# Scores of two groups in three by 32 keys on eight small tiles of the array in place of 64 keys on four, in a windowed attention and mixer kernel

## The chip, the core and the metric

The kernel runs on one core of a Trainium2 chip. The metric is the device time of one execution in microseconds. TensorE is called PE in the profile, VectorE DVE, ScalarE ACT, GpSimd POOL, SyncE SP.

## What is computed

The reference is an attention with a sliding window and a few sink keys, followed by an MLP mixer: first over tokens, then over channels. B, H, S, D are 4, 8, 768, 64; n_sink is 4 and window 128; the weights have 256 columns for tokens and 1536 for channels.

```python
scores = scale * np.matmul(q, k.transpose(0, 1, 3, 2))
keep = (pos[None, :] < n_sink) | ((rel >= 0) & (rel < window))   # rel = query - key
scores = np.where(keep, scores, -1000000000.0)
a = softmax(scores);  attn = a @ v
x = attn.transpose(0, 2, 1, 3).reshape(B, S, H * D)
xt = x.transpose(0, 2, 1)
h = np.maximum(xt @ w_tok1, 0.0) @ w_tok2
u = x + h.transpose(0, 2, 1)
out = u + np.maximum(u @ w_ch1, 0.0) @ w_ch2
```

## The kernel before

**Tiles.** Two heads of a batch are a pair; there are 16, pair p belonging to batch p // 4. The two heads (index i) lie in the two halves of 64 partitions of kT and qT, so a matmul for one head uses 64 rows of the array. S is six tiles of P = 128 (NT = 6). A key tile of 128 can only be seen by its own 128 queries and the next 128, so scores are kept as 128 keys by 256 queries; a group g is two such key tiles (k = 0, 1), and the groups 0, 1, 2 make a pair. The scores of one group fill one buffer of the tag "sc" in PSUM, `[P, i, k, 4, D]`: partitions are keys, then head, key tile, and 256 queries as four blocks of 64. There are two such buffers, and four banks of the tag "mx" for everything else.

**Scores** (`scores`, from line 547). The first four pairs, and group 0 of all pairs, go by_halves: for a key tile and a head one matmul with 64 rows and 128 keys as columns of the array, over 256 queries. Groups 1 and 2 of the pairs from 4 on go by_quarters: 64 keys are the columns (y = 0, 1), so that four tiles of 64x64 of the array work on the two heads and the two key halves, each over the 192 queries that can see its keys. The blocks that no matmul writes (the fourth for the first 64 keys, the first for the others) hold what was there; the exponential on ScalarE (line 587) reads all, and a multiplication by a 0/1 mask on VectorE (line 595) removes what is not kept. The last piece in the call of `piece` is the array's time in ns that the plan works with.

**Sink scores** (`score_sinks`, line 609). For two pairs at once, 32 keys of the first tile against queries 256 to 767: four matmuls on tiles of 64x32, 512 columns streamed.

**Turns.** q and k of pairs 5 to 7 are transposed by the array inside a burst (`transposed`, line 495) into a buffer of "sc" that is seen as bf16 (`turned_bank`), copied out, and then a memset clears one block of it (`cleared`, line 518), since its scores do not write that block. Pairs from 8 on are transposed by DMA from SP's queue. u of batch 1 is turned by the array in tiles of 64x64 (`turned_u` with `turn_quarters`, line 470), in the bursts of the scores of pairs 7 and 8; u of batches 2 and 3 goes by DMA transposes (`transfer_u`, line 853).

**Order.** Everything is emitted by a planner in the order in which each engine executes it. `first_attention` does the attention and token mixing of batch 0 by a list (FIRST_BATCH). Then there are two lists of units for TensorE: main, the channel mixers of batches 0 to 3 with 48 units each (24 of w_ch1, then 24 of w_ch2; a unit of w_ch1 is four matmuls over 384 columns), and side, the attention and token mixing of the batches 1 to 3 in 74 units. A burst is a side unit of several pieces, such as the scores of groups 1 and 2 of a pair, then turned u if there is any, then the sink scores if the pair's number is even. MERGED gives the order of the side units: "7/11" places unit 7 when 11 main units are out. `run` (line 338) takes each unit at the time at which the plan thinks that its inputs and PSUM banks are there, and gives the work that follows it (exponentials, copies, adds, loads) to the engine that is free first, by the costs written at each operation. On the chip each engine runs its instructions in this order and waits where an input is late.

**Loads.** POOL issues the loads of q, k (cast to bf16, two DMAs each), v and weights in the order of LOADS: T and A are w_tok1 and w_tok2, C0 to C3 quarters of w_ch1, D0 to D3 quarters of w_ch2. A load waits for its buffer (six of each of q, k, v).

Of the kernel before, what the change touches and what calls it, by code (L numbers as in the profile page):

```python
# [16 lines left out]
def kernel(  # L17
# [13 lines left out]
    nc = tc.nc  # L31
    B, H, S, D = q.shape
    P = 128
    NT = S // P
# [6 lines left out]
    NHP = H // 2  # L41
    HS = S // 2
    D1 = D + 1
# [1 line left out]


    MERGED = (
# [5 lines left out]
    )  # L53
    FIRST_BATCH = (
        "q0 k0 m00 s00 m01 s01 q1 m02 k1 s02 m11 x1 s11 m10 q2 s10 o01 m12 k2 s12 o00 m21 q3 s21 s20 k3 o11 "
# [1 line left out]
        "u21 t20 t30 u31 t31 t21"  # L57
    )
    LOADS = (
        "v1 v2 T0 v3 A0 k4 q4 C0 q5 C1 k5 q6 C2 k6 v4 v5 D0 q7 k7 C3 q8 v6 k8 D1 D2 D3 v7 q9 k9 v8 k10 v9 q10 "  # L60
        "v10 k11 q11 q12 q13 k12 k13 v11 k14 v12 q14 v13 v14 k15 q15 v15"
    )
    NQ = 6
    NPT = 3
# [17 lines left out]
    sc = [psum.tile([P, 2, 2, 4, D], FP32, name=f"ps_sc{n}", tag=f"sc{n}", bufs=1) for n in range(TAGS["sc"])]  # L82

    def bank(tag, *shape, dtype=FP32, slot=None):

        n = given[tag].pop(0) if slot is None else slot
        if tag == "sc":
            return sc[n]
        return psum.tile([P, *shape], dtype, name=f"ps_{tag}", tag=f"{tag}{n}", bufs=1)

    in_order = tc.keep_in_program_order
# [41 lines left out]
    def mm(*args, **kwargs):  # L133
        in_order(nc.tensor.matmul(*args, skip_group_check=True, **kwargs))  # L134
# [20 lines left out]
    tiles = {}  # L155
# [51 lines left out]
    ODD = D // 2  # L207
    v_sink_f = singles.tile([P, NHP, 2, D1], FP32)
    in_order(nc.vector.memset(v_sink_f, 0.0))  # L209
    for n in range(4):  # L210
        i, odd = n // 2, n % 2
        rows = slice(D * i + ODD * odd, D * i + ODD * odd + n_sink)
# [201 lines left out]
    def piece(ns, fn, deps, need, then, keys=()):  # L414
        op = Op({}, fn, deps, then, size=float(ns))
        op.need, op.keys = need, keys
        return op
# [100 lines left out]
    def cleared(key, readers):  # L518

        op = Op(  # L520
            {"DVE": 400.0}, lambda e: in_order(nc.vector.memset(tiles["ps_turned", key][0:D, :, :, 3], 0.0)), readers,
        )
        op.urgent = 2
        return op

    def width(g):
        return 3 * P if g == NT // 2 - 1 else 4 * P

    def of_keys(ps):
        return ps.rearrange("p i k b q -> p i (k b q)")  # L530
# [16 lines left out]
    def scores(p, g):  # L547

        by_pe = ("mask", p, g) in done
        quarters = p >= NHP and g > 0

        def by_halves(ps):
            for k in range(2):
                kt = 2 * g + k
                nq = 2 if kt < NT - 1 else 1
                for i in range(2):
                    mm(
                        of_keys(ps)[:, i, ds(2 * k * P, nq * P)], tiles["kT", p][ds(D * i, D), ts(kt, P)],  # L560
                        tiles["qT", p][ds(D * i, D), kt * P:(kt + nq) * P], start=not by_pe, stop=True,
                    )

        def by_quarters(ps):
            for k in range(2):
                for y in range(2):
                    a = 4 * g + 2 * k + y
                    nq = min(3, 2 * NT - a)
                    for i in range(2):
                        rows = ds(D * i, D)  # L570
                        mm(
                            ps[ds(D * y, D), i, k, y:y + nq], tiles["kT", p][rows, ts(a, D)],
                            tiles["qT", p][rows, D * a:D * (a + nq)], start=True, stop=True,
                        )

        def run():
            if ("pT", p) not in tiles:
                tiles["pT", p] = pTb[p % NPT]
            if not by_pe:
                tiles["ps_s", p, g] = bank("sc")  # L580
            (by_quarters if quarters else by_halves)(tiles["ps_s", p, g])

        def part(t):
            return t.rearrange("p i k n q -> p i (k n q)")[:, :, 0:width(g)]

        def exp(e):
            in_order(nc.scalar.activation(  # L587
                part(tiles["pT", p][:, :, ds(2 * g, 2)]), of_keys(tiles["ps_s", p, g])[:, :, 0:width(g)], AF.Exp,
                scale=scale,
            ))  # L590

        def mask(e):
            pt = part(tiles["pT", p][:, :, ds(2 * g, 2)])
            m = part(mask_first if g == 0 else mask_main)
            in_order(nc.vector.tensor_tensor(out=pt, in0=pt, in1=m, op=ALU.mult))  # L595

        x = done["exp", p, g] if by_pe else Op({}, None)
        x.cost, x.fn, x.deps = {"ACT": 190.0 + 1.5 * width(g)}, exp, [("pv", p - NPT)] if p >= NPT else []
        x.urgent = 2 * (p < NHP)
        then = [x]  # L600
        if not by_pe:
            then.append(Op({"DVE": 100.0 + 1.2 * width(g)}, mask, [x, done["masks"]]))
            then[-1].urgent = 2 * (p < NHP)
        done["p", p, g] = then[-1]
        deps = [*done["qT", p], *done["kT", p]] if g else [done["qT", p][0], done["kT", p][0]]
        deps += [done["mask", p, g]] if by_pe else []
        return piece((190, 165, 140)[g] if quarters else width(g) * 0.47, run, deps, {} if by_pe else {"sc": [[x]]}, then, [("s", p)])

    def score_sinks(p):


        def run():
            pT_sink = pTsb[p // 2 % 2]
            tiles["ps_sk", p] = bank("mx", (NT - 2) * P)
            for n in (p - 1, p):
                tiles["pT_sink", n] = pT_sink
                for i in range(2):
                    rows = ds(D * i, D)
                    c = ODD * (n % 2)
                    mm(  # L620
                        tiles["ps_sk", p][ds(D * i + c, ODD)], tiles["kT", n][rows, 0:ODD],
                        tiles["qT", n][rows, 2 * P:], start=True, stop=True,
                    )

        def exp(e):
            in_order(nc.scalar.activation(tiles["pT_sink", p], tiles["ps_sk", p], AF.Exp, scale=scale))

        x = Op({"ACT": 580.0}, exp, [("pv", n - 4) for n in (p - 1, p)] if p >= 4 else [])
        for n in (p - 1, p):
            done["p", n, NT] = x  # L630
        deps = [d for m in (p - 1, p) for d in [done["kT", m][0], *done["qT", m]]]
        return piece(320, run, deps, {"mx": [[x]]}, [x], [("sk", p - 1), ("sk", p)])

    def pv(p, half):
        b, hp = pairs[p]
# [251 lines left out]
    def first_attention():  # L887


        for p in range(NHP):  # L890
            prepare(p)
        made, names = {}, FIRST_BATCH.split()
        for p in range(NHP):
            for n in range(2):
                made["qk"[n] + str(p)] = turn(p, n)
        for p in range(NHP):
            for g in range(NT // 2):
                if f"m{p}{g}" in names:
                    made[f"m{p}{g}"] = masked(p, g)
                made[f"s{p}{g}"] = burst(scores(p, g))  # L900
            if p % 2:
                made[f"x{p}"] = burst(score_sinks(p))
                for n in (p - 1, p):
                    for half in range(2):
                        made[f"o{n}{half}"] = pv(n, half)
        for ct in range(NC):
            made[f"h{ct}"] = mix_h(0, ct, 0, NTOK)
            for half in range(2):
                by_pe = f"y{ct}{half}" in names
                made["uy"[by_pe] + f"{ct}{half}"] = mix_u(0, ct, half * QH, QH, by_pe)  # L910
                made[f"t{ct}{half}"] = transpose_u(0, ct, half * QH, QH)
        return [[made[name] for name in names]]

    def attention_and_tokens():
# [5 lines left out]
        for p in range(first, last + 1):  # L920
            b, hp = pairs[p]
            pieces = []
            if p < last:
                prepare(p + 1)
                if p + 1 < BY_DMA:
                    pieces.append(transposed(p + 1))
            pieces.append(scores(p, 0))
            if p > first:
                pieces.append(sink_values(p - 1))
# [6 lines left out]
            if p > first:  # L936
                units += [values(p - 1, i) for i in range(2)]
            pieces = [scores(p, 1), scores(p, 2)]
            if hp == 0 and p > first:
                units.append(mix_h(b - 1, 1, 0, NTOK))  # L940
# [228 lines left out]
```

## Time and profile before

| | us |
|---|---|
| median of 3 runs | 200.25 |
| lowest, highest | 199.9, 200.53 |
| the profiled execution, its own time | 200.4 |
| its span in the trace | 198.6 |

In the profile a busy time is the union of an engine's instructions, and PEld is the loading of weights, which runs beside the matmuls. A row of groups has the source line, engine, operation, output <- inputs by name, tile of the array (rows*columns), partitions x columns streamed, count, then busy us and mean ns of one, then idle time before them. Matmuls on different tiles of the array overlap, and a record holds the whole passage through the array, so the mean ns of one is longer than the step from one to the next. A few per cent of the matmul records can be missing. A row of the timeline has the start in us, the length from the first start to the last end, the group and its count (the shape named is that of the first). The chain is the work that ended last, followed back.

### The profile page before, as it was taken

The page shows a single profiled execution, that of the slowest core. Times are in us where ns is not written, and L with a number is a line of the kernel's source. Part 1 is how long each engine was busy: PE and PEld are TensorE (multiplying, and loading weights), DVE is VectorE, ACT ScalarE, POOL GpSimd, SP SyncE. Part 2 cuts the span into 40 slices and gives each one's busy share as a digit, 9 for nine tenths or more (in the row PEclk, how much of TensorE's full clock was granted, in tenths as well). Part 3 has the DMA queues.
Part 4 walks back from the last instruction along what each step waited for, and adds up shares of the span by engine and source line. Part 5 has one row for each costly group of instructions (what it writes and reads, how often), then busy time and mean ns, then how long its engine had stood idle before and what let it go on. Part 6 is the DMA issues. An engine that isn't in the chain of part 4 may idle for free.

```text
span 198.6 us, 4863 instructions
## 1 busy us (share of the span) xinstructions
PE 191.5 (96%) x2041; PEld 115.5 (58%) x2059; DVE 101.8 (51%) x224; ACT 105.5 (53%) x182; POOL 68.0 (34%) x86
## 2 busy tenths in 40 slices
PE   6998999999999999999999999999999999999993
PEld 1345995566655665566546755656655645564453
DVE  4578875688675465251646965606346431001222
ACT  4699767887735225887653554886610105772000
POOL 6099889779529624863530000000000000000000
PEclk9999999999999999999999999999999999999999
DMA  6999999999999999999999975100015161000223
GB/s 194 251 285 173 176 183 173 175 174 177 195 136 158 123 243 160 192 181 118 156 131 185 205 167 122 53 3 2 0 53 135 53 171 70 0 0 0 109 106 106
DMA packets 92358, 26.28 MB, mean 132 GB/s; under 512 B 82352, under 2 KB 89392, under 8 KB 92336
## 3 DMA queue, kind: packets, MB, share of 16 engines
q0 software_dynamic: 67232, 11.80, 76.5%
q1 hardware_dynamic: 25104, 14.17, 33.7%
q8 instruction: 16, 0.26, 0.5%
q14 instruction: 6, 0.05, 0.1%
HBM read 26.75 MB, written 6.29 MB: 166 GB/s over the span
## 4 chain that ended last, share of the span: by engine, by line
PE 90%; POOL 4%; DMA 3%; DVE 1%; issue 1%; SPq 1%; POOLq 0%
PE ps_mx L134 82%; PE ps_sc L134 5%; DMA v_sink_f<-in_v_dram 3%; POOL v_aug L127 2%; POOL w_tok L152 1%; PE ps_mx L137 1%; PE ps_sc L503 1%; SPq L213 1%; PE ps_mx L487 0%; PE ps_mx L475 0%; POOL k_bf L143 0%; POOL q_bf L143 0%; POOL v_sink L143 0%; DVE v_sink_f L209 0%; DVE mask_add L178 0%
## 5 line engine op out<-in xcount | busy, mean ns | idle before, releaser
L134 PE MATMUL ps_mx<-uT,w_ch 128*128 128x384 bf16 x384 | 66.6, 326 | 0.0
L134 PE MATMUL ps_mx<-w_ch,v1T 128*128 128x512 bf16 (+2 forms) x297 | 65.2, 362 | 0.9 <-issue 0.3
L587 ACT ACTIVATE pT<-ps_sc 128x1024 bf16<-128x1024 f32 (+1 forms) x48 | 44.2, 954 | 22.7 <-PE ps_sc L134 22.5
L147 ACT ACTIVATE v1T<-ps_mx 128x384 bf16<-128x384 f32 x80 | 39.3, 491 | 27.0 <-PE ps_mx L134 15.5
L134 PEld LDWEIGHTS <-w_ch 128*128 128x128 bf16 x384 | 36.0, 98 | 23.7 <-issue 0.9
L134 PEld LDWEIGHTS <-v1T 128*128 128x128 bf16 x312 | 28.5, 98 | 27.7 <-issue 0.5
L1005 DVE TENSOR_TENSOR o_sb<-ps_mx,u_sb 128x512 f32<-128x512 f32 x23 | 15.9, 691 | 40.9 <-PE ps_mx L134 38.9
L119 POOL DMA_DIRECT2D q_bf<-in_q_dram x24 | 19.9, 834 | 9.3 <-DMA v_aug<-in_v_dram 6.6
L119 POOL DMA_DIRECT2D k_bf<-in_k_dram x24 | 19.8, 831 | 7.8 <-DMA v_aug<-in_v_dram 2.0
L134 PEld LDWEIGHTS <-w_tok 128*128 128x128 bf16 x240 | 19.5, 98 | 4.8 <-issue 0.2
L804 DVE TENSOR_TENSOR u_sb<-ps_mx,x_sb 128x512 bf16<-128x512 f32 (+1 forms) x24 | 15.2, 655 | 13.1 <-PE ps_mx L134 13.1
L127 POOL DMA_DIRECT2D v_aug<-in_v_dram x16 | 16.8, 1052 | 9.7 <-PE ps_mx L134 5.5
L149 DVE TENSOR_SCALAR v1T<-ps_mx 128x384 bf16<-128x384 f32 x16 | 8.6, 550 | 19.9 <-PE ps_mx L134 19.7
L134 PEld LDWEIGHTS <-pT 128*128 128x128 bf16 x352 | 14.2, 98 | 2.7 <-issue 0.6
L595 DVE TENSOR_TENSOR pT<-pT,mask_main 128x768 bf16<-128x768 bf16 (+1 forms) x25 | 14.7, 615 | 1.3 <-ACT pT L587 1.2
L134 PE MATMUL ps_mx<-v_aug,pT 128*128 128x65 bf16 x352 | 15.3, 194 | 0.0
L134 PE MATMUL ps_sc<-qT,kT 64*64 64x192 bf16 (+3 forms) x288 | 15.1, 252 | 0.1
L134 PE MATMUL ps_mx<-h1T,w_tok 128*128 128x256 bf16 (+1 forms) x120 | 13.9, 252 | 0.1
L147 ACT ACTIVATE h1T<-ps_mx 128x512 bf16<-128x512 f32 (+1 forms) x9 | 4.5, 503 | 17.4 <-PE ps_mx L134 17.4
L134 PEld LDWEIGHTS <-kT 64*64 64x64 bf16 (+2 forms) x320 | 7.5, 101 | 10.6 <-issue 8.8
L134 PE MATMUL ps_mx<-x_sb,w_tok 128*128 128x256 bf16 (+1 forms) x120 | 12.2, 251 | 0.0
L697 DVE TENSOR_TENSOR x_sb<-ps_mx,recip 128x384 bf16<-128x384 f32 x22 | 11.6, 548 | 0.1
(64 smaller groups left out, 120.2 us busy)
## 6 DMA issues: line engine op xcount, KB each, us to landing
out_dram<-o_sb SPq DMA_DIRECT2D x23, 256.0 KB, 4.5
v_aug<-in_v_dram POOLq DMA_DIRECT2D x16, 192.0 KB, 10.4
w_ch<-in_moe_w_ch_dram POOLq DMA_DIRECT2D x8, 384.0 KB, 7.7
k_bf<-in_k_dram POOLq DMA_DIRECT2D x24, 96.0 KB, 8.2
q_bf<-in_q_dram POOLq DMA_DIRECT2D x24, 96.0 KB, 8.7
q_f<-in_q_dram SPq DMA_DIRECT2D x4, 384.0 KB, 6.0
k_f<-in_k_dram SPq DMA_DIRECT2D x4, 384.0 KB, 6.3
w_tok<-in_moe_w_tok_dram POOLq DMA_DIRECT2D x2, 384.0 KB, 7.3
```

The lines of the kernel that those rows point to most:

```text
L119: in_order(nc.gpsimd.dma_start(out=out[:, h], in_=rows[:, h]))
L127: in_order(nc.gpsimd.dma_start(out=v_aug.rearrange("p i t d -> p (i t) d")[:, :, 0:D], in_=v[b].rearrange("h s d -> (h s) d")[2 * hp * S:2 ...
L134: in_order(nc.tensor.matmul(*args, skip_group_check=True, **kwargs))
L137: in_order(nc.tensor.transpose(out, in_, ident))
L147: in_order(nc.scalar.activation(out, in_, AF.Relu))
L149: in_order(nc.vector.tensor_scalar_max(out=out, in0=in_, scalar1=0.0))
L152: return in_order(nc.gpsimd.dma_start(out=out, in_=in_))
L587: in_order(nc.scalar.activation(part(tiles["pT", p][:, :, ds(2 * g, 2)]), of_keys(tiles["ps_s", p, g])[:, :, 0:width(g)], AF.Exp, scale=scale,
L595: in_order(nc.vector.tensor_tensor(out=pt, in0=pt, in1=m, op=ALU.mult))
L697: in_order(nc.vector.tensor_tensor(out=x_sb[b][:, :, ds((2 * hp + i) * D, D)], in0=tiles["ps_o", p, i][:, :, 0:D], in1=tiles["recip", p, i ...
L804: in_order(nc.vector.tensor_tensor(out=u_part(b, g, s0, n), in0=tiles["ps_u", b, g, s0], in1=x_sb[b][:, s0:s0 + n, c0:c0 + cn], op=ALU.add,))
L1005: in_order(nc.vector.tensor_tensor(out=o_sb.rearrange("p (g c) -> p g c", g=2), in1=u_rows(b, st), in0=tiles["ps_out", b, st].rearrange("p ...
```

## The change

In groups 1 and 2 of the pairs from 4 on, 32 keys (ODD = D // 2) are the columns of the array instead of 64. A key tile is then four strips c of 32 keys, and with the two heads a set is eight matmuls on eight tiles of 64x32, each over the 160 queries that can see its keys (fewer at the end of the sequence). A burst of both groups has 32 matmuls where it had 16. The strip that the memset clears is now columns 160 to 255 of partitions 0 to 63. The plan's costs of a group 2 (140 to 125) and of sink scores (320 to 230 from pair 4 on) change, and MERGED and LOADS are new lists of the same units and loads.

```diff
@@ -45,11 +45,11 @@
 
 
     MERGED = (
-        "0/0 1/2 2/3 3/8 7/11 4/15 5/16 6/18 8/19 9/20 10/20 11/22 12/23 13/25 15/25 16/27 14/27 18/27 17/27 "
-        "19/31 20/35 22/36 21/36 23/39 25/41 24/41 26/41 27/44 28/55 31/57 30/58 29/58 32/68 33/70 34/72 "
-        "35/72 40/76 43/80 36/82 41/82 42/82 44/85 38/85 46/85 45/85 39/86 55/87 37/87 47/87 48/89 49/90 "
-        "51/90 50/90 52/95 54/96 53/96 59/96 67/109 56/114 57/115 58/115 60/118 61/120 64/120 65/121 63/126 "
-        "62/126 66/128 68/128 69/129 70/132 71/134 72/135 73/135"
+        "1/0 0/2 2/3 3/7 7/10 4/14 6/15 5/17 8/18 10/19 9/20 11/21 12/22 15/24 13/24 16/24 14/24 17/24 18/25 "
+        "19/27 20/34 22/37 21/37 23/40 25/42 26/42 24/42 27/45 31/48 28/58 30/60 29/60 32/70 34/72 35/72 "
+        "33/72 40/76 42/80 41/83 43/83 44/85 36/86 45/86 46/86 37/87 55/87 38/87 47/87 39/87 49/88 51/88 "
+        "48/88 50/89 52/91 54/93 53/95 59/97 56/104 58/106 57/106 64/112 67/114 65/114 60/114 61/116 66/120 "
+        "68/122 69/123 63/127 70/130 71/132 62/133 72/134 73/135"
     )
     FIRST_BATCH = (
         "q0 k0 m00 s00 m01 s01 q1 m02 k1 s02 m11 x1 s11 m10 q2 s10 o01 m12 k2 s12 o00 m21 q3 s21 s20 k3 o11 "
@@ -57,8 +57,8 @@
         "u21 t20 t30 u31 t31 t21"
     )
     LOADS = (
-        "v1 v2 T0 v3 A0 k4 q4 C0 q5 C1 k5 q6 C2 k6 v4 v5 D0 q7 k7 C3 q8 v6 k8 D1 D2 D3 v7 q9 k9 v8 k10 v9 q10 "
-        "v10 k11 q11 q12 q13 k12 k13 v11 k14 v12 q14 v13 v14 k15 q15 v15"
+        "v1 v2 T0 v3 A0 k4 q4 q5 C0 v4 k5 C1 v5 q6 C2 k6 C3 k7 q7 D0 q8 v6 k8 D1 D2 D3 v7 k9 q9 q10 v8 k10 "
+        "k11 q11 v9 v10 k12 k13 q12 q13 v11 v12 k14 q14 v13 k15 q15 v14 v15"
     )
     NQ = 6
     NPT = 3
@@ -518,7 +518,8 @@
     def cleared(key, readers):
 
         op = Op(
-            {"DVE": 400.0}, lambda e: in_order(nc.vector.memset(tiles["ps_turned", key][0:D, :, :, 3], 0.0)), readers,
+            {"DVE": 400.0}, lambda e: in_order(nc.vector.memset(of_keys(tiles["ps_turned", key])[0:D].rearrange(
+                "p i (k q) -> p i k q", k=2)[:, :, :, P + ODD:], 0.0)), readers,
         )
         op.urgent = 2
         return op
@@ -549,7 +550,7 @@
 
 
         by_pe = ("mask", p, g) in done
-        quarters = p >= NHP and g > 0
+        eighths = p >= NHP and g > 0
 
         def by_halves(ps):
             for k in range(2):
@@ -561,16 +562,16 @@
                         tiles["qT", p][ds(D * i, D), kt * P:(kt + nq) * P], start=not by_pe, stop=True,
                     )
 
-        def by_quarters(ps):
+        def by_eighths(ps):
             for k in range(2):
-                for y in range(2):
-                    a = 4 * g + 2 * k + y
-                    nq = min(3, 2 * NT - a)
+                for c in range(4):
+                    a = 4 * (2 * g + k) + c
+                    nq = min(P + ODD, S - ODD * a)
                     for i in range(2):
                         rows = ds(D * i, D)
                         mm(
-                            ps[ds(D * y, D), i, k, y:y + nq], tiles["kT", p][rows, ts(a, D)],
-                            tiles["qT", p][rows, D * a:D * (a + nq)], start=True, stop=True,
+                            of_keys(ps)[ds(ODD * c, ODD), i, ds(2 * P * k + ODD * c, nq)], tiles["kT", p][rows, ts(a, ODD)],
+                            tiles["qT", p][rows, ds(ODD * a, nq)], start=True, stop=True,
                         )
 
         def run():
@@ -578,7 +579,7 @@
                 tiles["pT", p] = pTb[p % NPT]
             if not by_pe:
                 tiles["ps_s", p, g] = bank("sc")
-            (by_quarters if quarters else by_halves)(tiles["ps_s", p, g])
+            (by_eighths if eighths else by_halves)(tiles["ps_s", p, g])
 
         def part(t):
             return t.rearrange("p i k n q -> p i (k n q)")[:, :, 0:width(g)]
@@ -604,7 +605,7 @@
         done["p", p, g] = then[-1]
         deps = [*done["qT", p], *done["kT", p]] if g else [done["qT", p][0], done["kT", p][0]]
         deps += [done["mask", p, g]] if by_pe else []
-        return piece((190, 165, 140)[g] if quarters else width(g) * 0.47, run, deps, {} if by_pe else {"sc": [[x]]}, then, [("s", p)])
+        return piece((190, 165, 125)[g] if eighths else width(g) * 0.47, run, deps, {} if by_pe else {"sc": [[x]]}, then, [("s", p)])
 
     def score_sinks(p):
 
@@ -629,7 +630,7 @@
         for n in (p - 1, p):
             done["p", n, NT] = x
         deps = [d for m in (p - 1, p) for d in [done["kT", m][0], *done["qT", m]]]
-        return piece(320, run, deps, {"mx": [[x]]}, [x], [("sk", p - 1), ("sk", p)])
+        return piece(320 if p < NHP else 230, run, deps, {"mx": [[x]]}, [x], [("sk", p - 1), ("sk", p)])
 
     def pv(p, half):
         b, hp = pairs[p]
```

## The prediction

> **What bounds the kernel now.** I read the page first: shares, the slices, the chain.
>
> ```profile
> span 198.6 us, 4863 instructions
> PE 191.5 (96%) x2041; PEld 115.5 (58%) x2059; DVE 101.8 (51%) x224; ACT 105.5 (53%) x182; POOL 68.0 (34%) x86
> ...
> PE   6998999999999999999999999999999999999993
> ...
> PEclk9999999999999999999999999999999999999999
> ...
> PE 90%; POOL 4%; DMA 3%; DVE 1%; issue 1%; SPq 1%; POOLq 0%
> ```
>
> TensorE is busy in every slice but the first and the last, at full clock, and is 90% of the chain that ended last; no other engine is above 53%. Next the waits of TensorE alone:
>
> ```profile
> engine line waited for: us in total, times, longest us
> PE ps_mx L134 <- DVE ones L161: 1.5, 1, 1.5
> PE ps_mx L487 <- POOL k_bf L143: 0.4, 1, 0.4
> PE ps_mx L487 <- DVE k_bf L143: 0.4, 1, 0.4
> PE ps_mx L134 <- issue: 0.3, 2, 0.2
> PE ps_mx L487 <- ACT q_bf L141: 0.3, 1, 0.3
> ```
>
> All of it is 2.9 us, 2.6 of them in the opening (line 161 is the memset before the first matmul, line 487 the first turns). So a nanosecond taken from the array in the stretch of the change comes off the end nearly whole, and a wait put in there is paid whole.
>
> What the array does there is read in the timeline of TensorE, around four bursts (pairs 4, 7 and 8; the last two rows give the rate of a long run):
>
> ```profile
> 36.15 0.49 PE L134 MATMUL ps_sc<-qT,kT 64*64 64x192 bf16 x16
> 36.57 0.40 PE L134 MATMUL ps_mx<-qT,kT 64*32 64x512 bf16 x4
> 36.90 2.12 PE L134 MATMUL ps_mx<-uT,w_ch 128*128 128x384 bf16 x12
> ...
> 60.30 0.49 PE L134 MATMUL ps_sc<-qT,kT 64*64 64x192 bf16 x16
> 60.61 0.60 PE L475 MATMUL ps_mx<-ident,u_sb 64*64 64x64 bf16 x48
> ...
> 73.82 0.60 PE L475 MATMUL ps_mx<-ident,u_sb 64*64 64x64 bf16 x48
> 74.35 0.40 PE L134 MATMUL ps_mx<-qT,kT 64*32 64x512 bf16 x4
> ...
> 164.19 15.76 PE L134 MATMUL ps_mx<-uT,w_ch 128*128 128x384 bf16 x96
> 179.79 15.76 PE L134 MATMUL ps_mx<-w_ch,v1T 128*128 128x512 bf16 x94
> ```
>
> Durations of single matmuls overlap, so I work from start to start. Ninety-six matmuls of 384 columns take 179.79 - 164.19 = 15.60 us: 162.5 ns each, 0.423 ns per column streamed. A scores burst is 16 matmuls of four tiles each, so four sets: three of 192 columns and one that its 128-column members end. Four tiles at once make that 3 x 81.3 + 54.2 = 298 ns; 60.30 to 60.61 is 310. So a set of four streams at once, its weight loads are hidden, and 12 ns at most is entry. The same burst before the sink scores takes 36.57 - 36.15 = 420 ns. The 110 ns more are the change of tile shape, 64x64 to 64x32. The sink scores' 512 columns need 217 ns, and 36.57 to 36.90 is 330: the next change of shape is 113 ns. Both agree; I take 0.11 us a change.
>
> **The change, part by part.**
>
> *Narrower tiles.* How many there are:
>
> ```profile
> L134 PE MATMUL ps_sc<-qT,kT 64*64 64x192 bf16 x144 | 5.3, 251 | 0.0
> L134 PE MATMUL ps_mx<-qT,kT 64*32 64x512 bf16 x32 | 3.2, 387 | 0.1
> L134 PE MATMUL ps_sc<-qT,kT 64*64 64x128 bf16 x24 | 2.6, 216 | 0.0
> L134 PE MATMUL ps_sc<-qT,kT 64*64 64x64 bf16 x24 | 2.3, 189 | 0.0
> ```
>
> The 192 matmuls are 12 bursts of 16. After, a burst is 32 matmuls and 32 loads in four sets of eight: three of 160 columns, and one that its two 128-column members end (the others have 96, 64, 32). If eight tiles stream at once, a set of 160 is 67.7 ns and the burst loses 3 x 13.5 = 41 ns: 12 x 41 = 0.49 us. The trace has no set of eight, so this is an estimate with two ends. Better: the entry of a load half as wide goes too, at most the 12 ns, 0.14 us in all. Worse: the queue can't bring 64 instructions fast enough. The fastest stream of small pairs is the 48 turns at 73.82: to 74.35 it is 530 ns, less 110 for the change of shape, 8.75 ns a pair; 32 pairs are 280 ns against 310, a gain of 0.36. I take 0.49, since the turns' streaming is itself 12 x 27 = 325 of their 420 ns, and the queue fills during the long matmuls ahead.
>
> The Trainium skill weighs in here: in "TensorE: Matmul & The Clock Gate", Part 3 (the measured speedup and span model), packed tiles cost their duration plus about 4 ns for each further tile. Taken once a burst, eight tiles instead of four cost 16 ns more, and the sum below would be 0.19 us smaller. Taken at each set, four tiles would have cost 48 ns in the 310, where the row leaves 12; so the trace agrees at most with once.
>
> *Changes of shape.* The sink scores are 64x32 already. In five of the six bursts that carry them (pairs 4, 6, 10, 12, 14) they follow the scores directly, and the change of 0.11 us goes: -0.55. In pairs 7 and 8 the turned u of batch 1 (line 475, 64x64) follows the scores. It followed in the same shape; now a change stands between, as 60.30 to 60.61 had none: +0.22. In pair 8 the sink scores still follow the turns and keep theirs. Bounds 90 to 113 ns a change (the upper one may hold the sink scores' own entry, as much again as the 12 ns above, and rounding): net -0.27 to -0.34; I take -0.33.
>
> *The clear.* The strip wiped behind a turned q and k (line 521) grows from 256 to 384 elements.
>
> ```profile
> 34.04 1.02 ACT L587 ACTIVATE pT<-ps_sc 128x1024 bf16<-128x1024 f32 x1
> 34.61 0.27 DVE L521 MEMSET ps_sc<- 64x256 f32 x1
> ...
> L521 DVE MEMSET ps_sc<- 64x256 f32 x3 | 0.8, 272 | 0.3
> ...
> L209 DVE MEMSET v_sink_f<- 128x520 f32 x1 | 0.5, 492 | 0.0
> ```
>
> From 256 to 520 elements it is 220 ns more, so 128 more are about 107 ns, three times. The matmul of the second strip writes columns 160 to 191 of partitions 32 to 63, which the wider clear also writes, so the array now waits for it, where only the exponential did. It ends at 34.88, would at 34.99, and the burst that takes the bank starts at 36.15, now one main unit (0.65 us) earlier: some 0.5 us remain, nothing on the path. Behind it on VectorE stand relus that are 0.1 us later, under the same cover. With the cover gone it is 3 x 0.1 us.
>
> *Loads in another order.* q5, v4, k5 and v5 move ahead of parts of w_ch1 (C0, C1, C2); nothing is added, and from q8 on the set that stands ahead is the same.
>
> ```profile
> 19.81 0.77 POOL L152 DMA_DIRECT2D w_ch<-in_moe_w_ch_dram  x1
> 20.56 1.64 POOL L119 DMA_DIRECT2D q_bf<-in_q_dram  x2
> 22.88 0.75 POOL L152 DMA_DIRECT2D w_ch<-in_moe_w_ch_dram  x1 [0.69 <-DMA w_tok<-in_moe_w_tok_dram]
> ...
> DMA to landing us min/median/max: 7.1/7.3/7.4
> ...
> 29.34 0.82 PE L134 MATMUL ps_mx<-uT,w_ch 128*128 128x384 bf16 x4
> ...
> 32.80 3.42 PE L134 MATMUL ps_mx<-uT,w_ch 128*128 128x384 bf16 x20
> ```
>
> (POOL's issues; the time to landing of w_ch; its first readers.) C0, behind q5's two casts, is issued at 21.45 and lands 7.3 later, 28.8, read from 29.34: 0.6 us remain of 2.2. C1 has v4 and k5 ahead as well, some 1.0 and 1.64: issued at 25.5, landed at 32.8. Its first reader is the seventh unit; 32.80 is the fourth, and units take 4 x 162.5 ns, so 34.75: 2 us remain. The q and k that move forward land earlier. I cost it at nothing; without that cover each microsecond late is one on the end.
>
> *Merged order.* The same 74 units of attention and token mixing go in among the same main units, most within three places of where they were. The array's work is unchanged and there is no stall here to win back, so the order is worth nothing at best; what it may cost is the first rival.
>
> **The sum.** -0.49 - 0.33 = -0.82 us. The profiled execution took 200.4 (span 198.6 and 1.8 around it); the median is 200.25, so 0.15 less. Span 197.8, that execution 199.6, median 199.45.
>
> **Rivals.**
>
> *A: the new order lets a wait in.* The tightest place that I find is u of batch 2, which goes to the channel mixer by DMA transposes (line 858):
>
> ```profile
> 113.47 1.44 SPq L858 DMA_TRANSPOSE uT<-u_sb  x1
> ...
> 117.60 2.58 SPq L858 DMA_TRANSPOSE uT<-u_sb  x2
> ...
> DMA to landing us min/median/max: 4.9/4.9/4.9
> ...
> 117.97 3.40 PE L134 MATMUL ps_mx<-w_ch,v1T 128*128 128x512 bf16 x15
> ...
> 123.92 1.31 PE L134 MATMUL ps_mx<-uT,w_ch 128*128 128x384 bf16 x7
> ```
>
> The last transpose is issued at 117.60 + 1.3 = 118.9, 0.93 after the last unit of u (117.97), and lands by that row at 123.8; the first reader is at 123.92. From that last unit to the reader both orders have about 5.95 us of work. But all of group 0's u now runs at main places 86 and 87, where it was spread over 82 to 87, and its transpose goes out about 2.5 us ahead of group 1's last unit instead of 4.5. SP issues the three in a row: 1.44, then 1.29, so the last goes out at about 118.97 + 0.2 and lands 0.1 us after the reader is due. If the transposes also share the engines, the shift of 2.0 us comes on top: a wait of 0.1 to 2.1. For it: the spare shown is only 0.1. Against it: a landing is inferred, and the true one may be earlier. At the middle, 1.1 us, the gain is gone: 200.5, and from a wait of 0.82 it is slower than before.
>
> *B: four small tiles in one row of the array do not stream at once.* It ends on the other side. The place is each set of eight: the 64 partitions of a head would feed four different stretches of q together, where quarters and sink scores feed two. If only two go at once, a set takes two turns: 135 ns for 81, three times, and 54 + 27 for 54 in the last, +188 ns a burst, 2.3 us in all, less 0.33 from the shapes: 202.2. It decides once a set takes over 90 ns, because then 12 x 3 x 9 ns eat the shapes' 0.33. Against it only that two do stream at once without loss. The Trainium skill is against it too ("TensorEngine Tiling (Array Packing)", Available Configurations and Key Properties: 64x32 gives eight tiles, and different tiles work in parallel); no row here shows a set of eight.
>
> *C: twice the weight loads are no longer hidden.* Eight loads fall in 68 ns where four fell in 81. If each set shows one load of 32 columns, 13.5 ns, it is 54 a burst and 0.65 us: 200.1, no change that can be told. Against it: in the 310 ns four sets with loads of 64 columns, 27 ns each, leave 12, so they hide now. The Trainium skill has a rule for it: in "TensorE: Matmul & The Clock Gate", Part 3 (what overlaps and what doesn't), a load overlaps a running matmul only in another group of rows. Each set here fills both groups of rows, so by that rule no set's loads would hide; the 12 ns disagree.
>
> **How the numbers follow.** My forecast 0.56, A 0.22, B 0.12, C 0.10. By the repeats of the kernel before, 0.3% or 0.6 us is about what a measurement can tell. Alone, my forecast runs from 199.1 (all bounds to the good, and 0.2 for the spread of a median) to 199.8 (slow queue, and the same). Faster by 0.3% means under 199.65: 0.50 of my case and 0.04 of A's. Within: 0.06 of mine, C, and 0.10 of A. Slower means over 200.85: 0.08 of A and B's 0.12. The range reaches from 198.9, a little under my case, to 200.9, which takes in C and A to its middle and leaves out B and the end of A.
>
> **What would show it.** In the timeline of TensorE, from a scores burst's first matmul to the sink scores' first about 0.27 us instead of 0.42, and from those to the next unit 0.33 as now; in pair 7 from the scores to the first turn about 0.38 instead of 0.31. The 64x64 rows of ps_sc gone, 384 matmuls of 64x32 in their place. The waits of TensorE as short as now. A burst of some 0.32 us before the sink scores would mean C; one over 0.45, B. A new line among TensorE's waits, or a gap ahead of the first uT reader of batch 1, 2 or 3, would be A. I am wrong if the bursts shrink as said and the end does not move: then the time went into a wait that I did not find.

## The result and the profile after

| | before | changed |
|---|---|---|
| median of 11 runs, us | 200.39 | 199.29 |
| lowest, highest | 199.74, 201.14 | 198.75, 200.22 |
| profiled execution: span | 198.6 | 197.7 |

The ratio is 0.9947, with a 95% interval of 0.9926 to 0.9968: 1.06 us less, between 0.64 and 1.48 (the two medians differ by 1.10). The forecast was 0.82 less, 199.45 (199.29 came out).

The page of the changed kernel, the lines that answer to those of before:

```profile
span 197.7 us, 5262 instructions
PE 190.7 (96%) x2251; PEld 114.5 (58%) x2251; DVE 102.6 (52%) x218; ACT 106.6 (54%) x188; POOL 67.6 (34%) x86
...
PE   6798999999999999999999999999999999999993
...
PE 88%; DMA 7%; POOL 1%; DVE 1%; SPq 0%; issue 0%; POOLq 0%
```

TensorE is as full as before and the end has come nearer by 0.9. Of the 399 further instructions 192 are loads and 210 are matmuls, 18 of them records that the first trace lacked; other kinds have 3 fewer. The longest waits of TensorE:

```profile
PE ps_mx L134 <- DVE ones L161: 1.5, 1, 1.5
PE ps_mx L487 <- POOL k_bf L143: 0.7, 1, 0.7
PE ps_mx L487 <- DVE k_bf L143: 0.6, 2, 0.3
...
```

These and the four shorter ones belong to the opening (the memset of line 161, the casts and copies of the first pairs). None is in the stretch of the change.

The timeline of TensorE in the changed kernel, the same bursts as in the prediction (pairs 4, 5, 7, 8) and the first unit of batch 3:

```profile
29.35 0.82 PE L134 MATMUL ps_mx<-uT,w_ch 128*128 128x384 bf16 x4
...
35.51 0.44 PE L134 MATMUL ps_sc<-qT,kT 64*32 64x160 bf16 x32
35.78 0.40 PE L134 MATMUL ps_mx<-qT,kT 64*32 64x512 bf16 x4
36.12 2.12 PE L134 MATMUL ps_mx<-uT,w_ch 128*128 128x384 bf16 x12
38.17 0.44 PE L134 MATMUL ps_sc<-qT,kT 64*32 64x160 bf16 x32
38.54 0.66 PE L134 MATMUL ps_mx<-uT,w_ch 128*128 128x384 bf16 x3
...
57.39 0.44 PE L134 MATMUL ps_sc<-qT,kT 64*32 64x160 bf16 x32
57.76 0.58 PE L475 MATMUL ps_mx<-ident,u_sb 64*64 64x64 bf16 x48
...
73.86 0.44 PE L134 MATMUL ps_sc<-qT,kT 64*32 64x160 bf16 x32
74.23 0.58 PE L475 MATMUL ps_mx<-ident,u_sb 64*64 64x64 bf16 x48
74.74 0.40 PE L134 MATMUL ps_mx<-qT,kT 64*32 64x512 bf16 x4
75.07 0.61 PE L134 MATMUL ps_mx<-w_ch,v1T 128*128 128x512 bf16 x2
...
163.27 15.76 PE L134 MATMUL ps_mx<-uT,w_ch 128*128 128x384 bf16 x96
```

The row of pair 5 before, which the prediction did not show, and the unit behind it:

```profile
38.95 0.49 PE L134 MATMUL ps_sc<-qT,kT 64*64 64x192 bf16 x16
39.38 0.34 PE L134 MATMUL ps_mx<-uT,w_ch 128*128 128x384 bf16 x1
```

A burst of scores alone, from its first matmul to the next unit, went from 0.43 us to 0.37. One with the sink scores went from 36.90 - 36.15 = 0.75 to 36.12 - 35.51 = 0.61. In pair 8, with turns and sink scores, 1.17 (73.51 to 74.68) became 1.21.

The best ruler is the stretch of the merged order, from the start of the first main unit to the start of the first one of batch 3, because it leaves the opening out: 164.19 - 29.34 = 134.85 before, 163.27 - 29.35 = 133.92 after. That is 0.93 less, and the whole gain of this pair of executions. The opening differs from execution to execution, 28.7 to 29.6 us to the first main unit over all traces, which is one reason why the medians need many runs.

### The profile page after: what moved, and what is told of

It is laid out like the page before. It is cut to its first block, busy times and chain, and to the rows that moved or that the text cites. A ratio compares the mean times of both kernels' runs of the same rounds, so it can differ in the third digit from the quotient of the medians.

```text
span 197.7 us, 5262 instructions
## 1 busy us (share of the span) xinstructions
PE 190.7 (96%) x2251; PEld 114.5 (58%) x2251; DVE 102.6 (52%) x218; ACT 106.6 (54%) x188; POOL 67.6 (34%) x86
## 4 chain that ended last, share of the span: by engine, by line
PE 88%; DMA 7%; POOL 1%; DVE 1%; SPq 0%; issue 0%; POOLq 0%
PE ps_mx L134 82%; PE ps_sc L134 4%; DMA w_tok<-in_moe_w_tok_dram 4%; DMA v_sink_f<-in_v_dram 3%; POOL v_aug L127 1%; PE ps_mx L137 1%; PE ps_sc L503 1%; PE ps_mx L475 1%; SPq L213 0%; POOL v_sink L143 0%; PE ps_mx L487 0%; DVE v_sink_f L209 0%; DVE mask_add L178 0%; DVE ones L161 0%; DVE v_aug L195 0%
## 5 line engine op out<-in xcount | busy, mean ns | idle before, releaser
L134 PE MATMUL ps_mx<-w_ch,v1T 128*128 128x512 bf16 (+2 forms) x312 | 67.2, 363 | 0.0
L147 ACT ACTIVATE v1T<-ps_mx 128x384 bf16<-128x384 f32 x82 | 40.3, 492 | 29.6 <-PE ps_mx L134 18.1
L149 DVE TENSOR_SCALAR v1T<-ps_mx 128x384 bf16<-128x384 f32 x14 | 7.6, 550 | 18.9 <-PE ps_mx L134 18.8
L134 PEld LDWEIGHTS <-pT 128*128 128x128 bf16 x352 | 14.7, 98 | 4.0 <-issue 1.0
L134 PE MATMUL ps_mx<-v_aug,pT 128*128 128x65 bf16 x352 | 16.1, 193 | 0.0
L134 PE MATMUL ps_sc<-qT,kT 64*32 64x160 bf16 (+3 forms) x480 | 14.0, 232 | 0.2 <-ACT kT L141 0.2
L134 PEld LDWEIGHTS <-kT 64*32 64x32 bf16 (+1 forms) x512 | 7.1, 91 | 9.1 <-issue 7.8
```

The costliest lines, as they stand in the source:

```text
L147: in_order(nc.scalar.activation(out, in_, AF.Relu))
L149: in_order(nc.vector.tensor_scalar_max(out=out, in0=in_, scalar1=0.0))
```

## The experiments

The theory before them: the gain is the bursts' own, shorter sets and fewer changes of tile shape, and the new order is worth nothing. The rivals: the order has a share; the pace of a set is not set by streaming; a change of shape costs less than taken. All numbers of a stretch are differences of two rows as above.

| kernel | ratio to before (95%) | stretch, us | first main unit at |
|---|---|---|---|
| before, three traces | | 134.85, 135.54, 134.95 | 29.34, 28.71, 29.39 |
| changed, two traces | 0.9947 (0.9926 to 0.9968) | 133.92, 133.91 | 29.35, 29.34 |
| tiles only, two traces | 0.9968 (0.9944 to 0.9992) | 134.17, 134.16 | 28.73, 29.32 |
| order only | 1.0006 (0.9982 to 1.003) | 134.84 | 29.00 |
| tiles and loads, two traces | 0.9924 (0.9895 to 0.9953) | 133.95, 133.93 | 29.55, 29.11 |
| fewer shapes | 0.9935 (0.9912 to 0.9959) | 133.80 | 29.06 |
| two shapes | 1.002 (1.0 to 1.0039) | 135.59 | 29.42 |
| wide strips | 0.996 (0.9932 to 0.9988) | 134.27 | 29.29 |
| narrow strips | 0.9893 (0.986 to 0.9925) | 133.29 | 29.17 |

**Tiles only.** The kernel before with by_eighths and the wider clear; MERGED, LOADS and the plan's costs as they were.

> Tiles of 64x32 and the wider clear in the kernel before; MERGED, LOADS and the plan's costs stay as before. Theory (the gain is the bursts' own: 41 ns of streaming and 12 ns of entry in each of 12, five changes of shape gone, two added): about 0.9 us less than before, ratio 0.995 to 0.996, bursts as in the changed kernel, no new wait of TensorE. Rival (part of the gain, or what made it possible, is the new order): less than 0.5 us, or a new wait of TensorE.

Measured: 0.64 us less, and 0.68 in the stretch instead of 0.93. The bursts are those of the changed kernel, but 0.25 us of waits stand between them: 0.18 ahead of the unit behind pair 5 (38.74 - 38.19 = 0.55 for 0.37), and 0.07 ahead of the first reader of C3, which lands as that unit starts (issued at 36.84, 8.1 us to landing, 44.94). So the rival has something.

**Order only.** The changed kernel with `(by_quarters if eighths else by_halves)` and the old clear; its order, loads and costs stay.

> The changed kernel with 64 keys on four tiles and the old clear; its MERGED, LOADS and plan costs stay. Theory: the order is worth nothing, ratio 0.999 to 1.001, span 198.5 to 198.7. Rival (the order has a share): 0.3 us or more to either side.

Measured: no difference in the time, and 134.84 in the stretch, the same as the kernel before in its one trace without waits (134.85).

**The wait of tiles only.** My first explanation was chance: the array came to the stretch 0.6 us earlier in that execution than before, and the loads did not. So the same kernel again, the changed kernel again, and the tiles with the new LOADS but the old MERGED and costs.

> The kernel with the tiles alone once more (old MERGED, LOADS and costs), for its trace. In its first trace the opening was short (first main unit at 28.73 us) and 0.25 us of waits stood in the stretch from there to batch 3 (134.17). Theory (loads land by the clock of the DMA engines, so the old loads are late only if the array comes early): with the first main unit at 29.3 or later the stretch is 133.9 to 134.0, earlier than 29.0 it is 134.1 or more. Rival (the old merged order costs 0.25 in any case): 134.1 or more with a late opening too.

> The changed kernel once more, for a second trace. Theory: the stretch from the first main unit to batch 3 is 133.9 whether the opening is short or long, since no load in it is near its reader. Rival: a short opening gives it waits as well, 134.1 or more.

> The kernel before with the tiles of 64x32, the wider clear and the new LOADS; MERGED and the plan's costs stay as before. In the run with the tiles alone the first reader of the last quarter of w_ch1 waited 0.07 us and one unit 0.18 for a relu behind the copies of v's sink rows, with the array 0.6 us earlier than in the profile before. Theory (the old loads are what was late): both waits gone, the stretch from the first main unit to batch 3 about 133.9 us as in the changed kernel. Rival (the old merged order is at fault): waits of 0.2 us or more remain, stretch 134.1 or more.

> The kernel with the tiles and the new loads, old MERGED and costs, once more. In its first trace the opening was long (29.55) and the stretch 133.95. Theory (the new loads are what keeps the waits out): 133.9 to 134.0 also with the first main unit before 29.0. Rival (the old merged order too has to be late): 134.1 or more with a short opening.

The theory of the early array falls: with the first main unit at 29.32 the stretch of tiles only is again 134.16. With the new LOADS it is 133.95 and 133.93, and the changed kernel has 133.91 again. VectorE and TensorE in the second trace of tiles only, around the scores of pair 5:

```profile
38.40 0.36 DVE L143 COPY v_sink<-v_aug 4x65 bf16<-4x65 bf16 x2 [1.90 <-DMA v_aug<-in_v_dram]
...
38.79 0.44 PE L134 MATMUL ps_sc<-qT,kT 64*32 64x160 bf16 x32
38.80 0.56 DVE L149 TENSOR_SCALAR v1T<-ps_mx 128x384 bf16<-128x384 f32 x1
...
39.41 0.97 PE L134 MATMUL ps_mx<-uT,w_ch 128*128 128x384 bf16 x5 [0.18 <-DVE v1T L149]
```

VectorE sits idle for 1.90 us until v4 has landed, to copy its sink rows (line 143). Behind these copies in its order stands a relu of the channel mixer (line 149), which ends at 39.36, and the next main unit needs the bank that it empties. From 38.79 to that unit it is 0.62 where 0.37 is undisturbed: 0.25 us, the whole difference. The same place with tiles and new loads, in its second trace:

```profile
37.38 0.56 DVE L149 TENSOR_SCALAR v1T<-ps_mx 128x384 bf16<-128x384 f32 x1 [0.63 <-PE ps_mx L134]
...
38.58 0.44 PE L134 MATMUL ps_sc<-qT,kT 64*32 64x160 bf16 x32
...
38.95 0.82 PE L134 MATMUL ps_mx<-uT,w_ch 128*128 128x384 bf16 x4
39.02 0.37 DVE L143 COPY v_sink<-v_aug 4x65 bf16<-4x65 bf16 x2
```

v4 is loaded ahead of C1 now, and VectorE's order comes out otherwise: the copies stand behind the relu, wait for nothing, and the unit follows 0.37 after the burst's first matmul. The shortest opening among the four traces with the new tiles and the new loads is 29.11, so the opening before 29.0 that the last expectation asked for was not met.

Whether the old loads are late only with the shorter bursts was still open, so the kernel before ran twice more.

> The kernel before once more, for its trace: behind the scores of pair 5 its relu had 0.48 us of spare, the tiles alone use 0.2 of it, and the landing of v4 moves by half a microsecond from one execution to another. Theory (the wait of tiles only needs the shorter bursts): stretch 134.85 and no wait there. Rival (v4's landing alone can do it, with the old tiles too): stretch 134.9 to 135.1, the unit behind pair 5 more than 0.43 after the burst's first matmul.

> The same kernel, a third trace, with the same two expectations: 134.85, or 134.9 to 135.1 with a wait behind pair 5.

The loads are late with the old tiles too: the rival holds, though 134.9 to 135.1 was too little for the second trace. That trace has a wait for k5 that no other trace has, 0.4 us long (0.60 from start to start), and the wait behind pair 5 in small:

```profile
PE ps_sc L503 <- DMA k_bf<-in_k_dram: 0.4, 1, 0.4
```

```profile
38.43 0.37 DVE L143 COPY v_sink<-v_aug 4x65 bf16<-4x65 bf16 x2 [2.08 <-DMA v_aug<-in_v_dram]
...
38.83 0.56 DVE L149 TENSOR_SCALAR v1T<-ps_mx 128x384 bf16<-128x384 f32 x1
38.92 0.49 PE L134 MATMUL ps_sc<-qT,kT 64*64 64x192 bf16 x16
...
39.44 1.30 PE L134 MATMUL ps_mx<-uT,w_ch 128*128 128x384 bf16 x7
```

39.44 - 38.92 is 0.52 where 0.43 is undisturbed. The stretch is 135.54, and an opening 0.6 us shorter is lost again in it. So the execution that the prediction was worked out on was one without these waits. In the third trace they are 0.10 in all (134.95): 0.03 behind pair 5 and 0.07 for C3, issued at 37.52 and landed 8.1 us later, 45.6, with its first reader at 45.65. The new LOADS have C3 earlier too. With them and the new tiles, no wait stands in the stretch in any of four traces.

**Two shapes.** `by_quarters if eighths and g == 1 else by_eighths if eighths else by_halves`: one more change of shape in each burst, and two sets of 192 columns.

> The changed kernel with group 1 on 64 keys and four tiles and group 2 on 32 keys and eight, so that each of the 12 bursts has one more change of shape. Theory (a change costs about 0.09 us plus an entry of 0.01, whatever the two shapes): two sets at 82 ns for 69 and 0.10 a burst, with 0.014 for the entry: 12 x 0.14 = 1.7 us over the changed kernel, 0.7 over the one before, ratio 1.003 to 1.004. Rival (what the sink scores saved was mostly their own entry, a change between small shapes is cheap): 12 x 0.03 to 0.06 = 0.4 to 0.7 us over the changed kernel, still faster than before.

```profile
38.36 0.59 PE L134 MATMUL ps_sc<-qT,kT 64*64 64x192 bf16 x24
38.88 0.66 PE L134 MATMUL ps_mx<-uT,w_ch 128*128 128x384 bf16 x3
```

Measured: 1.67 us over the changed kernel in the stretch, as the theory has it, and not faster than before. A burst alone is 38.88 - 38.36 = 0.52 instead of 0.37; less 2 x 13.5 ns of streaming and 13 of entry (both under "Narrower tiles" below), a change between the two small shapes is 0.11 us. In the five bursts where the sink scores follow directly it is less: 36.31 - 35.57 = 0.74 for 0.61.

**Wide strips.** `nq = min(P + 2 * ODD, S - ODD * a, 2 * P - ODD * c)`.

> The changed kernel, but each strip of 32 keys is scored over 192 queries as the strips of 64 were (160 for the fourth strip, which ends at the tile's border); the extra scores are masked out behind. Shapes and instructions stay. Theory (streaming sets the pace of a set of eight): three sets of a burst go from 69 to 82 ns, the burst ahead of the sink scores from 0.275 to 0.315, 0.48 us over the changed kernel in the stretch of the merged order. Rival (the queue's pace, 8 pairs at 8.7 ns = 70 ns, sets it): the sets stay near 70 and nothing moves by over 0.15.

Measured: 0.35 us over the changed kernel in the stretch, where the theory had 0.48 and the rival at most 0.15. Bursts alone grow from 0.37 to 38.54 - 38.13 = 0.41 (below), the 3 x 13.5 ns of streaming. Bursts with the sink scores only go from 0.61 to 36.07 - 35.45 = 0.62, and that is what is missing from the 0.48: by the single records (one for each matmul, which the timeline merges) the sink scores begin 28 ns later, but the next unit follows them 15 ns sooner (319 for 334).

```profile
35.45 0.48 PE L134 MATMUL ps_sc<-qT,kT 64*32 64x192 bf16 x32
...
36.07 2.12 PE L134 MATMUL ps_mx<-uT,w_ch 128*128 128x384 bf16 x12
38.13 0.48 PE L134 MATMUL ps_sc<-qT,kT 64*32 64x192 bf16 x32
38.54 0.66 PE L134 MATMUL ps_mx<-uT,w_ch 128*128 128x384 bf16 x3
```

**Narrow strips.** `nq = min(3 * ODD, S - ODD * a)`: 64 of the 160 queries of each strip are left out.

> The changed kernel, but each strip of 32 keys is scored over only 96 of its 160 queries; the rest of the scores is left out. It looks for the floor under a set of eight. Theory of streaming alone: 96 columns are 41 ns, the burst ahead of the sink scores 0.18. Rival (a pace of the queue of 8.4 to 8.7 ns a pair binds below 160 columns): sets near 68, burst 0.26 to 0.28, no gain; narrower strips would then be worth nothing.

```profile
35.33 0.35 PE L134 MATMUL ps_sc<-qT,kT 64*32 64x96 bf16 x32
35.57 0.41 PE L134 MATMUL ps_mx<-qT,kT 64*32 64x512 bf16 x4
...
37.97 0.35 PE L134 MATMUL ps_sc<-qT,kT 64*32 64x96 bf16 x32
38.25 0.66 PE L134 MATMUL ps_mx<-uT,w_ch 128*128 128x384 bf16 x3
```

Both were half right. A burst alone falls to 0.28, 0.09 less, where streaming gives 3 x 27 + 13 = 94 ns: 32 pairs are no bound even at 96 columns. But the sink scores begin 0.24 after their burst's first matmul where 0.18 was due. The 32 pairs ahead of them are not slower for it: they take 0.35 in both rows. The turns of pairs 7 and 8, which follow 32 pairs as well, take 57.90 - 57.36 = 0.54 and 74.36 - 73.78 = 0.58 here, where the changed kernel has 0.51. By the single records the four sink matmuls start 8 to 9 ns apart, where the eight of a set start 3 to 4 ns apart; the last three do so in the changed kernel too, and none in the kernel before. So streaming sets the pace of the sets of the change, and something delays the 33rd pair and after. A reading that fits is that the queue has some 32 pairs ready and brings the next at 7.5 to 9 ns a pair (0.24 / 32 is 7.5). No row shows the queue, so the cause stays argued.

**Fewer shapes.** In pair 8 `pieces.insert(2, score_sinks(p + 1))` puts the sink scores ahead of the turned u; pair 7 keeps by_quarters.

> The changed kernel with two edits: in pair 8 the sink scores go ahead of the turned u, and pair 7 keeps 64 keys on four tiles ahead of its turned u. Theory: pair 8 loses one change of shape (0.10 us), pair 7 loses one (0.10) and gains 0.05 of streaming and entry: 0.15 us less than the changed kernel, span 197.5. Rival: u of batch 1 is turned 0.33 us later and the first unit of its channel mixer waits for the copies: no gain, and a gap ahead of it.

Measured: 133.80 in the stretch, 0.12 less than the changed kernel where the theory had 0.15, and the shortest of the kernels that compute all; no new gap ahead of batch 1's first unit. In pair 8 the burst is 74.67 - 73.55 = 1.12 where the changed kernel has 1.21, in pair 7 57.95 - 57.11 = 0.84 for 58.27 - 57.39 = 0.88:

```profile
57.11 0.49 PE L134 MATMUL ps_sc<-qT,kT 64*64 64x192 bf16 x16
57.42 0.60 PE L475 MATMUL ps_mx<-ident,u_sb 64*64 64x64 bf16 x48
57.95 0.60 PE L134 MATMUL ps_mx<-w_ch,v1T 128*128 128x512 bf16 x2
...
73.55 0.44 PE L134 MATMUL ps_sc<-qT,kT 64*32 64x160 bf16 x32
...
74.67 0.60 PE L134 MATMUL ps_mx<-w_ch,v1T 128*128 128x512 bf16 x2
```

In time its ratio to before is 0.9935, its interval overlaps the changed kernel's, and 0.12 us is too little for the times to show.

## Why the prediction was right, step by step

**The bound.** Right: what the bursts lost, the stretch lost.

**Narrower tiles, -0.49.** Eight tiles do stream at once; rivals B (a burst over 0.45 ahead of the sink scores) and C (0.32) are out, since it is 0.27, the forecast number. Wide and narrow strips show that columns set the pace. The size was low: by the single records of the trace a burst alone lost 54 ns, 41 of streaming and 13 of entry, 0.65 in all. The entry was named as a bound to the good, 12 ns at most, and costed at nothing. Its place shows in the records of pair 4: the four sets start 107, 82 and 83 ns apart before, and 80, 70 and 69 after. The first step is longer by 25 ns before and by some 11 after, so the entry was twice the 12 ns read from 310 - 298, and some 13 of it went. (In pair 7 the first turn starts 35 ns after the last set, not the 54 that the 298 counts, which hid the rest.)

**Changes of shape, -0.33.** Right in kind; the price of a change, 0.11, is what two shapes gave. But by the single records a burst with the sink scores lost 142 ns, 54 of them the sets', so only 88 ns came of a change that went. Some 15 of the missing 22 ns stand behind the sink scores: from them to the next unit it is 334 ns, and 319 with two shapes and with wide strips. The queue, as read from the narrow strips, would explain that; it is not shown. In pair 8 the burst grew by 34 ns, 54 less for the sets and 88 more for the new change, since the turns behind it run some 25 shorter (74.74 - 74.23 = 0.51, before 74.35 - 73.82 = 0.53). Net 3 x 0.088 = -0.26, just short of the stated -0.27 to -0.34. With the entry, -0.65 - 0.26 = -0.91 for a measured -0.93. The two errors of size, +0.07 and -0.16, partly cancelled against -0.82, so that 199.29 came so near to 199.45 is in part luck.

**The clear.** 379 ns were worked out, and it takes 378; nobody waits for it.

```profile
L521 DVE MEMSET ps_sc<- 64x384 f32 x3 | 1.1, 378 | 0.4
```

**Loads, at nothing.** This step failed, in both directions. C0's spare of 0.6 us, seen from one execution, is used up in another: in the second trace of the changed kernel the first weight load of w_ch (PEld) waits 0.24 us for it, in the opening.

```profile
29.33 0.11 PEld L134 LDWEIGHTS <-w_ch 128*128 128x128 bf16 x2 [0.24 <-DMA w_ch<-in_moe_w_ch_dram]
```

And "there is no stall here to win back", said of the merged order, held for one execution of before and not for the other two, which have 0.69 and 0.10 of waits in the stretch, for k5 and v4 in the one and for v4 and C3 in the other. The new LOADS bring all three forward. With the new tiles they are worth 0.23 in the stretch (tiles only against tiles and loads). How much they are worth with the old tiles is not settled: order only has no wait in the stretch of its trace, and its time can't be told from before within 0.3%. The new MERGED is worth nothing that can be seen, since tiles and loads, with the old one, has the stretch of the changed kernel. That the time fell by 1.06 and the stretch of the first two traces by 0.93 fits the waits that other executions of before have, but the interval holds both, and it is not shown.

**Rival A.** It did not come, and its place was misread. In the kernel (`mix_channels`) the first three units of a batch read tokens 0 to 383 alone, and the last of the three transposes brings tokens 512 to 767. So its first reader is the fourth unit, three times 0.65 us behind the first, and the spare was about 2 us where I had counted 0.1. The second trace of before shows it: the last transpose lands at 119.0 + 5.2 = 124.2, and the first units run through from 123.98 without a wait.

```profile
L858 SPq DMA_TRANSPOSE uT<-u_sb x1: 1224/1224/1224, 119.0 to 119.0; - x1
DMA to landing us min/median/max: 5.2/5.2/5.2
...
123.98 3.26 PE L134 MATMUL ps_mx<-uT,w_ch 128*128 128x384 bf16 x19
```

SP's queue and the first reader of batch 2 in the changed kernel (from three views: SP, time to landing, TensorE):

```profile
114.21 1.44 SPq L859 DMA_TRANSPOSE uT<-u_sb  x1
...
117.12 2.57 SPq L859 DMA_TRANSPOSE uT<-u_sb  x2
...
DMA to landing us min/median/max: 3.3/3.3/3.3
...
122.36 0.81 PE L134 MATMUL ps_mx<-uT,w_ch 128*128 128x384 bf16 x4
```

The last transpose goes out at 118.5 and lands 3.3 us later, 121.8, ahead even of the first unit. The transposes did come closer together (2.9 us from the first to the second, 4.1 before), and it cost nothing. Had it landed as late as before, 4.9 us, 123.4 would still be ahead of the fourth unit. Why the landing took 4.9 to 5.2 us in three traces of before and 3.3 to 3.4 in two of the changed kernel is not shown.

## What to carry to other kernels

Count the changes of tile shape between neighbouring pieces along with the columns streamed. Here, where TensorE hardly waits, they were 0.09 to 0.11 us each, so that giving two neighbours one shape was worth twice the 41 ns for which a burst's sets were made narrower. A trace without a wait is one execution without a wait: where a load lands within half a microsecond of its reader, look at a second and a third trace before costing a new load order at nothing, and look for the reader behind the reader, in the order of an engine that is half idle. Check in the kernel which part of a tile its first reader reads before you count a spare. Measure such a change in a stretch of the trace that leaves the noisy part out; there 0.02 us separates two traces of a kernel without waits, where single times differ by over a microsecond.

## What was not expected of the hardware

In the narrow strips 32 pairs of small loads and matmuls on eight tiles pass without delay, and the matmuls behind them start late and 8 to 9 ns apart; that they wait for the queue is a reading, not shown. And the landing of a load moves by half a microsecond between executions of one kernel (v4's copies start at 37.94 in the first trace of before and at 38.43 in the second), while everything on TensorE between two waits repeats to 0.02.
